# Attention with two dense layers behind it: the product with v of a group in one stretch behind the scores

## The chip, the core and the metric

One core of one Trainium2 chip runs the whole program. The metric is the device time of one execution in microseconds (us), as the median of three runs. The engines are TensorE (PE; its weight loads are PEld), VectorE (DVE), ScalarE (ACT), GpSimd (POOL) and SyncE (SP, which here issues DMAs).

## What is computed

Attention with a threshold on the scores, for 4 batches and 8 heads of 576 rows of 64, and two dense layers over the 2304 rows that come out:

```
scores = q @ k.T / sqrt(64)
scores = where(scores >= max(scores) - tau, scores, -1e9)
attn = exp(scores - max); attn = attn / (sum(attn) + 1e-9)
x = (attn @ v) as 2304 x 512
h = x @ w_in;  g = where(h >= 1, h, where(h <= -1, 0, (h + 1)**2 / 4));  x = g @ w_out
h = x @ w_in2; g = h * clip(h + 3, 0, 6) / 6;                             out = g @ w_out2
```

## The kernel before

Attention runs over 16 jobs, each one batch and two heads. A job has five blocks of query rows: four of 128 rows a head, and a last one with the 64 remaining rows of both heads. For each block `em_scores` computes the scores on TensorE (L285, four matmuls, each with 64 rows of the array and 288 columns, into the PSUM pairs P0 and P1). VectorE copies them out with their maximum (L297), ScalarE takes the exponential (L301), and VectorE applies the threshold and sums (L307). One step later `em_pt` transposes these probabilities on TensorE (L245) and ScalarE evicts them into the tile `Gf` (L328). Two steps later `em_tail` transposes the last 64 keys of both heads into `Gt` (L342, L346).

The five blocks make two groups: "a" is blocks 0 and 1 (256 columns), "b" is blocks 2 to 4 (320 columns). For a group `pv_chunk` multiplies with v in five chunks of 128 keys, and each chunk is two matmuls, one for each head (L362): head 0 writes partitions 0 to 63 of the PSUM bank Q1, head 1 partitions 64 to 127, so each uses 64 columns of the array. The first four chunks read `Gf`, the fifth `Gt`. A group is thus ten matmuls; all are float32, and the trace holds two records for each of them. The chunks wait in the list `pvq` and `pv_run(n)` takes up to n of them. After the fifth, ScalarE copies the result into `xu` (L368). Then `em_norm` transposes the row sums into a PSUM pair (L395, L397), VectorE multiplies `xu` by them (L399, L403), and the result goes to HBM (`xd`), from where the dense layers read it (`xst`). `em_norm` also loads the v of the job after the next (L237, L238).

`attention` walks over the 80 blocks, one step each, and yields between its parts. From the step on in which the first four jobs are through, each yield lets the loop outside lay a share of the first dense layer between (`dense1`: L486 is its first product, L548 its second, both float32r with 256 columns, from `em_h` and `em_part`). In the same time the weights are split into two parts on ScalarE, VectorE and GpSimd (L111 to L137, from w_raw to wih, wil, woh, wol). When attention is through, the dense layers go on alone with 512 columns.

The order on each engine is not the order of the code alone: the framework orders instructions when the program is built, by their dependencies and by when it thinks that each can start, and `after(mm, prev)` pins one TensorE instruction behind another. A chunk of the product with v is pinned, for head 0, behind the last entry of `pe_pins` (the first instruction of the last transposes or scores), and head 1 behind head 0.

Of the kernel before, what the change touches and what calls it, by code (L numbers as in the profile page):

```python
# [18 lines left out]
def kernel(  # L19
# [54 lines left out]
    def bank(tag):  # L74
        return ps.tile([128, 512], F32, tag=tag, name=tag)
# [20 lines left out]
    def after(ins, prev):  # L96
        if prev is not None:
            tc.add_manual_dep(ins.ins, prev.ins.name, mybir.DependencyInfo(
                mybir.DependencyClass.NoSync, mybir.DependencyReason.DATA), reason="pace")

    pe_pins = []
# [91 lines left out]
    AFTER = {1: "a", 4: "b"}  # L193
# [46 lines left out]
    def unit_bank():  # L240
        mode["s"] += 1
        return pair_bank(f"P{mode['s'] % 2}")

    def turn(out, in_, pin):
        x = T.transpose(out, in_, ident)  # L245
        if pin:
            pe_pins.append(x)

    def unit_q(j):
        if j >= NJ:  # L250
            return
        tm = unit_bank().rearrange("p e n -> p (e n)")
        for c in range(5):
            turn(tm[:, c * 128:(c + 1) * 128], qn[:, c, :], c == 0)
        load_q(j + 1)
        qt[j] = ap.tile([128, SEQ], F32, tag="qt", name="qt", bufs=2)
        S.activation(out=qt[j], in_=tm[:, 0:SEQ], func=ACTF.Copy, scale=taus[:, 1:2])
# [10 lines left out]
        S.activation(out=kt[j], in_=tm[:, 128 - TAIL:128 + MAIN + TAIL], func=ACTF.Copy)  # L268

    zt, gt, xu, p_t = {}, {}, {}, {}  # L270

    def em_scores(j, i):

        last = i == NBLK - 1

        if not last:
            mode["s"] += 1
        ss = [unit_bank() for _ in range(1 if last else 2)]
        prev = None
        c = slice(i * 128, i * 128 + (TAIL if last else 128))  # L280
        for x, (h, e) in enumerate(((0, 0), (1, 1), (0, 1), (1, 0)) if last else ((0, 0), (1, 0), (0, 1), (1, 1))):
            r = slice(h * D, (h + 1) * D)
            k0 = e * HS + (TAIL if last or h == 0 else 0)
            o = ss[0][h * TAIL:(h + 1) * TAIL, e, 0:HS] if last else ss[h][:, e, 0:HS]
            mm = T.matmul(o, qt[j][r, c], kt[j][r, k0:k0 + HS], start=True, stop=True, skip_group_check=True)  # L285
            after(mm, prev)
            prev = mm
            if x == 0:
                pe_pins.append(mm)
        nm = ap.tile([128, 2], F32, tag="nm", name="nm", bufs=3)  # L290
        th = ap.tile([128, 2], F32, tag="th", name="th", bufs=3)
        p = ap.tile([128, 2, 2, HS], F32, tag="p", name="p", bufs=3)
        if i == 0:
            zt[j] = ap.tile([128, 9], F32, tag="z", name="z", bufs=2)
        es = []
        for x, s in enumerate(ss):
            V.tensor_scalar(out=p[:, x], in0=s[:, :, 0:HS], scalar1=-1.0, scalar2=3e38,  # L297
                            op0=ALU.mult, op1=ALU.min, accum_out=nm[:, x:x + 1])
        for x, s in enumerate(ss):
            e = ap.tile([128, 2, HS], F32, tag="e", name="e", bufs=3)  # L300
            pins["S"] = S.activation(out=e, in_=p[:, x], func=ACTF.Exp, bias=nm[:, x:x + 1], scale=-1.0)  # L301
            es.append(e)
        n = len(ss)
        V.tensor_scalar(out=th[:, 0:n], in0=nm[:, 0:n], scalar1=taus[:, 0:1], scalar2=None, op0=ALU.add)
        for x, e in enumerate(es):
            z = ZCOL[x](i)
            V.scalar_tensor_tensor(out=p[:, x], in0=p[:, x], scalar=th[:, x:x + 1], in1=e,  # L307
                                   op0=ALU.is_le, op1=ALU.mult, accum_out=zt[j][:, z:z + 1])
        p_t[j, i] = p.rearrange("p h e n -> p (h e n)")
# [24 lines left out]
    def em_tail(j, i):  # L334

        p = p_t.pop((j, i))
        g, d0 = PARTS[i]
        t = gt[g, j][1]
        tl = bank("Q0" if mode["mlp"] else "Q3")
        if i < NBLK - 1:  # L340
            turn(tl[:, 0:128], p[:, MAIN:MAIN + 128], True)
            S.activation(out=t[:, d0:d0 + 128], in_=tl[:, 0:128], func=ACTF.Copy)  # L342
        else:
            turn(tl[0:TAIL, 0:128], p[:, MAIN:SEQ], True)
            for x in HEADS:
                S.activation(out=t[x * TAIL:(x + 1) * TAIL, d0:d0 + TAIL],  # L346
                             in_=tl[0:TAIL, x * TAIL:(x + 1) * TAIL], func=ACTF.Copy)

    o_t, pvq = {}, []

    def pv_chunk():

        j, g, c = pvq.pop(0)
        n, d0 = GROUPS[g]
        f, t = gt[g, j]
        if c == 0:
            if j not in xu:
                xu[j] = ap.tile([128, SEQ], F32, tag="xu", name="xu", bufs=2)
            o_t[j, g] = bank("Q1")
        o = o_t[j, g][:, 0:n]  # L360
        for h in HEADS:
            mm = T.matmul(o[h * D:(h + 1) * D], vn[j % 2][:, c, h, :], f[:, h, c] if c < 4 else t,  # L362
                          start=(c == 0), stop=(c == 4), skip_group_check=True)
            after(mm, pe_pins[-1] if h == 0 else prev)
            prev = mm
        if c == 4:
            del gt[g, j], o_t[j, g]
            S.activation(out=xu[j][:, d0:d0 + n], in_=o, func=ACTF.Copy)  # L368

    def pv_run(n):  # L370
        for _ in range(min(n, len(pvq))):
            pv_chunk()
# [3 lines left out]
    def pre_norm(j):  # L376
        z = zt.pop(j)
        rz = ap.tile([128, 9, 1], F32, tag="rz", name="rz", bufs=2)
        V.tensor_scalar(out=z, in0=z, scalar1=1e-9, scalar2=None, op0=ALU.add)
        V.reciprocal(out=rz[:, :, 0], in_=z)  # L380
        rb = ap.tile([128, 4, 2, 64], F32, tag="rb", name="rb")
        for h, z0 in ((0, 0), (1, 5)):
            G.tensor_scalar(out=rb[:, :, h, :], in0=rz[:, z0:z0 + 4, :].to_broadcast([128, 4, 64]),
                            scalar1=1.0, scalar2=0.0, op0=ALU.mult, op1=ALU.add)
        rbs[j] = (rz, rb)

    def em_norm(j):
        while any(x[0] == j for x in pvq):
            pv_chunk()
        load_v(j + 2)  # L390
        b, hp = jobs[j]
        rz, rb = rbs.pop(j)
        bm = unit_bank().rearrange("p e n -> p (e n)")
        for c in range(4):
            T.transpose(bm[:, c * 128:(c + 1) * 128], rb[:, c].rearrange("p h n -> p (h n)"), ident)  # L395
        bt = bm[:, 512:640]
        T.transpose(bt, rz[:, 4, :].to_broadcast([128, 128]), ident)  # L397
        x = xu.pop(j)
        V.tensor_tensor(out=x[:, 0:MAIN], in0=x[:, 0:MAIN], in1=bm[:, 0:MAIN], op=ALU.mult)  # L399
        nc.sync.dma_start(out=xd[b][:, hp, :], in_=x[:, 0:MAIN])  # L400
        for h in HEADS:
            r = slice(64 * h, 64 * h + 64)
            V.tensor_tensor(out=x[r, MAIN:SEQ], in0=x[r, MAIN:SEQ], in1=bt[r, 64 * h:64 * h + 64], op=ALU.mult)  # L403
        nc.sync.dma_start(out=xd[NB][:, hp, b * TAIL:(b + 1) * TAIL], in_=x[:, MAIN:SEQ])
# [3 lines left out]
    def attention():  # L408

        order = [(j, i) for j in range(NJ) for i in range(NBLK)]  # L410
        n = len(order)
        for t in range(n + 3):
            mode["t"] += 1
            mode["step"] = True
            j, i = order[t] if t < n else (NJ, t - n)
            if t < n:
                em_scores(j, i)
                yield
            if 2 <= t < n + 2:
                em_tail(*order[t - 2])  # L420
            pv_run(3)
            yield
            if i == 0 and j:
                pre_norm(j - 1)
            if i == 2 and j:
                em_norm(j - 1)
                done_jobs.add(j - 1)
                yield
            if i == 3:
                unit_q(j + 1)  # L430
                yield
            if i == 4:
                unit_k(j + 1)
                yield
            if 1 <= t < n + 1:
                j, i = order[t - 1]
                em_pt(j, i, 0)
                yield
            pv_run(2)
            if 1 <= t < n + 1:  # L440
                if i < NBLK - 1:
                    em_pt(j, i, 1)
                    yield
                if i in AFTER:
                    pvq.extend((j, AFTER[i], c) for c in range(5))


    xs, gs, acc, cnt = {}, {}, {}, {"h": 0, "a": 0}
# [157 lines left out]
    while o < len(outs):  # L606
        n = len(steps)
# [138 lines left out]
    for _ in attention():  # L746
# [11 lines left out]
        while credit > 0:  # L758
            c = next(part1)
# [98 lines left out]
```

## Time and profile before

| | |
|---|---|
| median of three runs | 1183.13 us (1182.69 to 1183.19) |
| the profiled execution | 1181.81 us, span 1180.0 us |
| mean granted TensorE clock | 0.993 |
| TensorE matmuls busy | 1133.5 us (96%) |
| weight loads busy | 907.5 us (77%) |
| ScalarE, VectorE, GpSimd busy | 631.2, 581.4, 412.3 us |

Busy is the time in which at least one instruction of the engine was in work; matmuls overlap, so their own durations say less than the distance from one start to the next. The rows below are of that one execution.

### The profile page before, as it was taken

How to read it: one execution, taken by the hardware profiler on the slowest of the kernel's cores; microseconds unless marked ns; L12 is line 12 of the kernel's file. 1: busy time of each engine (PE TensorE's matmuls, PEld its weight loads, DVE VectorE, ACT ScalarE, POOL GpSimd, SP SyncE). 2: the span in 40 equal slices, each digit the busy share in tenths (PEclk: the TensorE clock that was granted, in tenths of full speed). 3: DMA queues.
4: the chain of work that ended last, by engine and by line, in shares of the span. 5: the costliest groups of instructions: out<-in, count | busy, mean ns of one | idle time of the engine just before them, and what ended most of it. 6: DMA issues, size and time to landing. Idle time of an engine off the chain costs nothing.

```text
span 1180.0 us, 17986 instructions
## 1 busy us (share of the span) xinstructions
PE 1133.5 (96%) x6680; PEld 907.5 (77%) x6680; DVE 581.4 (49%) x1208; ACT 631.2 (53%) x1234; POOL 412.3 (35%) x388
## 2 busy tenths in 40 slices
PE   8888799989999999999999999999999999999998
PEld 5555576667777777787888988888888888888886
DVE  5888876765565555535543666556631121121111
ACT  5666777755566656655664776645532232233222
POOL 0322663511111011113762756657833222222221
PEclk9999999999999999999999999999999999999999
DMA  5333344322212112004422245443210010010000
GB/s 132 88 93 92 108 139 126 109 62 71 69 52 60 40 41 58 21 20 124 146 90 72 87 147 160 149 146 98 72 50 9 1 60 8 1 46 1 18 1 36
DMA packets 110056, 85.59 MB, mean 73 GB/s; under 512 B 66704, under 2 KB 93840, under 8 KB 109968
## 3 DMA queue, kind: packets, MB, share of 16 engines
q1 hardware_dynamic: 108608, 84.14, 24.3%
q8 instruction: 53, 0.87, 0.3%
q10 hardware_dynamic: 1360, 0.30, 0.1%
q14 instruction: 35, 0.29, 0.1%
HBM read 66.06 MB, written 18.35 MB: 72 GB/s over the span
## 4 chain that ended last, share of the span: by engine, by line
PE 82%; ACT 5%; DVE 5%; DMA 4%; issue 2%; POOL 1%; ACTq 0%; SPq 0%; DVEq 0%; POOLq 0%
PE Q L486 33%; PE P L528 26%; PE Q L548 6%; PE Q L362 6%; PE P L285 5%; PE Q L245 5%; DVE p L297 2%; ACT e L301 1%; DVE p L307 1%; DMA xst<-xd 1%; PE P L245 1%; DMA xd<-xu 1%; ACT Gf L328 1%; DMA w_raw<-in_moe_w_out_dram 1%; ACT r L495 1%
## 5 line engine op out<-in xcount | busy, mean ns | idle before, releaser
L504 POOL TENSOR_TENSOR gl<-r,gh 128x512 fp32r<-128x512 f32 (+1 forms) x190 | 205.8, 1083 | 587.0 <-ACT gh L503 574.5
L486 PE MATMUL Q<-xh,wih 128*128 128x512 f32 (+1 forms) x760 | 265.2, 350 | 5.2 <-DVE r L497 3.9
L486 PE MATMUL Q<-xl,wih 128*128 128x512 f32 (+1 forms) x760 | 257.5, 339 | 0.6 <-DVE xl L470 0.5
L486 PE MATMUL Q<-xh,wil 128*128 128x512 f32 (+1 forms) x760 | 257.4, 339 | 0.0
L500 DVE SCALAR_TENSOR_TENSOR r<-r,Q 128x512 f32<-128x512 f32 (+1 forms) x80 | 50.7, 634 | 249.1 <-ACT r L499 248.9
L486 PEld LDWEIGHTS Q<-xh,wih 128*128 128x128 f32 x760 | 144.6, 190 | 37.2 <-issue 10.3
L503 ACT ACTIVATE gh<-r 128x512 fp32r<-128x512 f32 (+1 forms) x190 | 99.8, 525 | 119.6 <-PE P L528 53.1
L486 PEld LDWEIGHTS Q<-xl,wih 128*128 128x128 f32 x760 | 144.6, 190 | 16.7 <-DVE xl L470 1.0
L486 PEld LDWEIGHTS Q<-xh,wil 128*128 128x128 f32 x760 | 144.4, 190 | 15.4
L297 DVE TENSOR_SCALAR_CACHE_REDUCE p<-P 128x576 f32<-128x576 f32 x144 | 104.1, 754 | 70.8 <-PE Q L245 54.3
L307 DVE SCALAR_TENSOR_TENSOR p<-p,th,e 128x576 f32<-128x576 f32 x144 | 125.5, 886 | 25.0 <-ACT e L301 18.3
L245 PE MATMUL Q<-ident,p 128*128 128x128 f32 (+1 forms) x656 | 112.9, 287 | 19.2 <-ACT Gf L328 9.6
L301 ACT ACTIVATE e<-p,nm 128x576 f32<-128x576 f32 x144 | 109.6, 773 | 38.2 <-DVE p L297 36.9
L499 ACT ACTIVATE r<-Q,three 128x512 f32<-128x512 f32 (+1 forms) x80 | 51.4, 643 | 143.7 <-PE Q L486 140.6
L245 PEld LDWEIGHTS Q<-ident,p 128*128 128x128 f32 (+1 forms) x656 | 74.9, 142 | 57.5 <-ACT Gf L328 14.9
L497 DVE SCALAR_TENSOR_TENSOR r<-r,Q 128x256 f32<-128x256 f32 (+1 forms) x110 | 55.0, 500 | 119.0 <-ACT r L496 118.5
L285 PE MATMUL P<-kt,qt 64*128 64x288 f32 (+1 forms) x640 | 103.7, 432 | 10.3 <-DVE p L297 4.4
L528 PE MATMUL P<-woh,gh 128*128 128x512 f32 x288 | 111.9, 390 | 0.6 <-DVE ob L586 0.6
L528 PE MATMUL P<-wol,gh 128*128 128x512 f32 x288 | 112.2, 390 | 0.0
L528 PE MATMUL P<-woh,gl 128*128 128x512 f32 x288 | 111.0, 390 | 0.0
L130 POOL TENSOR_TENSOR w_c<-w_c,w_raw 128x512 int32<-128x512 int32 x64 | 90.5, 1414 | 39.8 <-DVE w_c L128 33.2
L328 ACT ACTIVATE Gf<-Q 128x512 f32<-128x512 f32 x128 | 75.0, 590 | 47.6 <-PE Q L245 47.4
(83 smaller groups left out, 1870.7 us busy)
## 6 DMA issues: line engine op xcount, KB each, us to landing
w_raw<-in_moe_w_in_dram SPq DMA_DIRECT2D x32, 512.0 KB, 3.9
w_raw<-in_moe_w_out_dram SPq DMA_DIRECT2D x32, 512.0 KB, 3.7
xst<-xd SPq DMA_DIRECT2D x32, 256.0 KB, 3.4
kn<-in_k_dram SPq DMA_DIRECT2D x32, 128.0 KB, 2.6
vn<-in_v_dram SPq DMA_DIRECT2D x32, 128.0 KB, 2.6
xd<-xu SPq DMA_DIRECT2D x16, 256.0 KB, 2.5
x2p<-ob SPq DMA_DIRECT2D x16, 256.0 KB, 2.5
x2d<-ob SPq DMA_DIRECT2D x16, 256.0 KB, 3.7
```

Of the source, the lines that this page charges most:

```text
L130: x = G.tensor_tensor(out=c.bitcast(I32), in0=c.bitcast(I32), in1=r, op=ALU.add)
L245: x = T.transpose(out, in_, ident)
L285: mm = T.matmul(o, qt[j][r, c], kt[j][r, k0:k0 + HS], start=True, stop=True, skip_group_check=True)
L297: V.tensor_scalar(out=p[:, x], in0=s[:, :, 0:HS], scalar1=-1.0, scalar2=3e38, op0=ALU.mult, op1=ALU.min, accum_out=nm[:, x:x + 1])
L301: pins["S"] = S.activation(out=e, in_=p[:, x], func=ACTF.Exp, bias=nm[:, x:x + 1], scale=-1.0)
L307: V.scalar_tensor_tensor(out=p[:, x], in0=p[:, x], scalar=th[:, x:x + 1], in1=e, op0=ALU.is_le, op1=ALU.mult, accum_out=zt[j][:, z:z + 1])
L328: S.activation(out=f[:, h, :, d0:d0 + 128], in_=tm.rearrange("p (c n) -> p c n", c=4), func=ACTF.Copy)
L362: mm = T.matmul(o[h * D:(h + 1) * D], vn[j % 2][:, c, h, :], f[:, h, c] if c < 4 else t, start=(c == 0), stop=(c == 4), skip_group_check=True)
L486: mm = T.matmul(h, l[:, kk * 128:(kk + 1) * 128], r, start=(x == 0), stop=(x == 3 * KD - 1))
L503: x = S.activation(out=gh, in_=r, func=ACTF.Copy)
L504: y = G.tensor_tensor(out=gl, in0=r, in1=f32(gh), op=ALU.subtract)
L528: T.matmul(a, l, r, start=(first and x == 0), stop=(last and x == 2))
```

## The change

The chunks of a group are entered in the list one step later, after `em_tail` of its last block, so that all five are there at once. `pv_run(5)` stands right behind `em_scores`, ahead of the yield, in place of `pv_run(3)` and `pv_run(2)` in two later places of the step. The pin of head 0 is now the last matmul of the scores (`last_score`), or the last matmul of the chunk before. The loop has one step more for it.

```diff
@@ -268,6 +268,7 @@
     zt, gt, xu, p_t = {}, {}, {}, {}
+    last_score = [None]
 
@@ -287,6 +288,7 @@
             if x == 0:
                 pe_pins.append(mm)
+        last_score[0] = prev
         nm = ap.tile([128, 2], F32, tag="nm", name="nm", bufs=3)
@@ -361,8 +363,9 @@
                           start=(c == 0), stop=(c == 4), skip_group_check=True)
-            after(mm, pe_pins[-1] if h == 0 else prev)
+            after(mm, last_score[0] if h == 0 else prev)
             prev = mm
+        last_score[0] = prev
@@ -409,16 +412,19 @@
-        for t in range(n + 3):
+        for t in range(n + 4):
             mode["t"] += 1
             mode["step"] = True
             j, i = order[t] if t < n else (NJ, t - n)
             if t < n:
                 em_scores(j, i)
-                yield
+            pv_run(5)
+            yield
             if 2 <= t < n + 2:
-                em_tail(*order[t - 2])
-            pv_run(3)
+                jt, it = order[t - 2]
+                em_tail(jt, it)
+                if it in AFTER:
+                    pvq.extend((jt, AFTER[it], c) for c in range(5))
             yield
@@ -436,13 +442,10 @@
                 em_pt(j, i, 0)
                 yield
-            pv_run(2)
             if 1 <= t < n + 1:
                 if i < NBLK - 1:
                     em_pt(j, i, 1)
                     yield
-                if i in AFTER:
-                    pvq.extend((j, AFTER[i], c) for c in range(5))
```

What this does to the order on TensorE is shown at two places. The first is group b of the first job, in the stretch with attention alone, before (P is a score, Q with p a transpose of probabilities, Q with Gf or Gt the product with v; x6 is six matmuls in a row):

```order
L285 MATMUL P_414<-kt,qt 128x288
L362 MATMUL Q_442<-Gf,vn_96 64x320 x6
L245 MATMUL Q_451<-ident,p 128x128 x4
L362 MATMUL Q_442<-Gf,vn_96 64x320 x2
L362 MATMUL Q_442<-Gt,vn_96 64x320 x2
L245 MATMUL Q_462<-ident,p 128x128 x4
L245 MATMUL Q_492<-ident,p 128x128
```

The same group now, where the product stands one block of scores later:

```order
L286 MATMUL P_457<-kt,qt 128x288
L364 MATMUL Q_474<-Gf,vn_96 64x320 x8
L364 MATMUL Q_474<-Gt,vn_96 64x320 x2
L245 MATMUL Q_510<-ident,p 128x128 x4
L245 MATMUL Q_516<-ident,p 128x128 x4
L398 MATMUL P_499<-ident,rb 128x128 x4
L400 MATMUL P_499<-ident,rz 128x128
```

All ten matmuls are in one stretch behind the scores, and the transposes for the normalisation (L398) come soon after. The second place is group b of the eighth job, in the stretch where dense work lies between, before:

```order
L245 MATMUL Q_3022<-ident,p 64x128
L362 MATMUL Q_3026<-Gf,vn_97 64x320 x6
L245 MATMUL Q_3035<-ident,p 128x128 x4
L362 MATMUL Q_3026<-Gf,vn_97 64x320 x2
L362 MATMUL Q_3026<-Gt,vn_97 64x320 x2
L395 MATMUL P_3077<-ident,rb 128x128 x4
```

and now (L551 is the dense product that was L548):

```order
L551 MATMUL Q_2859<-gh,wol_2644 128x256
L364 MATMUL Q_3058<-Gf,vn_97 64x320
L245 MATMUL Q_3022<-ident,p 64x128
L364 MATMUL Q_3058<-Gf,vn_97 64x320 x7
L245 MATMUL Q_3028<-ident,p 128x128 x4
L364 MATMUL Q_3058<-Gt,vn_97 64x320 x2
L398 MATMUL P_3077<-ident,rb 128x128 x4
```

The six and four have become one, seven and two, and the product doesn't stand behind scores.

At the end of attention, between the last matmul of the product with v and the first matmul with 512 columns, there are 33 narrow dense matmuls before and 24 now. Counted over the whole order, the 32 groups stand on TensorE like this (a stretch is a run of matmuls of one group with nothing between; a lone head more is one that has no partner in its stretch, counted in pairs of them; an end at scores is a stretch that begins right behind scores or ends right ahead of them):

| groups | stretches before, now | pairs before, now | ends at scores before, now |
|---|---|---|---|
| first 8, attention alone | 16, 8 | 41, 40 | 9, 8 |
| next 9 (108 to 280 us before) | 19, 29 | 46, 54 | 2, 9 |
| last 15 (280 to 535 us before) | 30, 47 | 75, 92 | 0, 9 |

A pair here is what two heads side by side take, and a lone head counts as one pair too: five of the eight added in the middle line, and eight of the seventeen in the last, are of 256 columns, the others of 320.

## Rows read from the trace of the kernel before

**Rows 1.** Busy us (records) of PE, PEld, DVE, ACT, POOL; clock; DMA share, GB/s.

```profile
0.00:108.00 108.00, 92.32 (x612) 58.44 (x613) 79.97 (x213) 68.78 (x138) 25.16 (x41) 0.97 0.38 100
108.00:280.00 172.00, 151.62 (x1084) 114.24 (x1084) 123.47 (x287) 121.59 (x261) 75.65 (x76) 0.98 0.38 109
280.00:535.00 255.00, 250.78 (x1871) 194.57 (x1871) 136.23 (x376) 154.14 (x337) 34.91 (x51) 1.00 0.16 44
```

**Rows 2.** TensorE's timeline: start, us, instruction, records [idle before].

```profile
99.00 1.24 PE L285 MATMUL P<-kt,qt 64*128 64x288 f32 x8
100.17 1.83 PE L362 MATMUL Q<-Gf,vn 128*64 128x320 f32 x12
101.93 1.24 PE L285 MATMUL P<-kt,qt 64*128 64x288 f32 x8
...
106.68 1.24 PE L285 MATMUL P<-kt,qt 64*128 64x288 f32 x8
107.85 0.66 PE L245 MATMUL Q<-ident,p 128*128 128x128 f32 x4
...
116.07 0.65 PE L362 MATMUL Q<-Gf,vn 128*64 128x256 f32 x4
116.55 0.60 PE L362 MATMUL Q<-Gt,vn 128*64 128x256 f32 x4
117.08 1.19 PE L285 MATMUL P<-kt,qt 64*64 64x288 f32 x8
```

**Rows 3.** TensorE's timeline at a group that stands in three pieces.

```profile
276.63 0.65 PE L362 MATMUL Q<-Gf,vn 128*64 128x256 f32 x4
277.11 0.59 PE L362 MATMUL Q<-Gt,vn 128*64 128x256 f32 x2
277.64 0.39 PE L486 MATMUL Q<-xh,wih 128*128 128x256 f32 x1
...
278.94 0.28 PE L486 MATMUL Q<-xl,wih 128*128 128x256 f32 x1
279.06 0.28 PE L486 MATMUL Q<-xh,wil 128*128 128x256 f32 x1
279.27 0.65 PE L362 MATMUL Q<-Gt,vn 128*64 128x256 f32 x2
279.84 0.38 PE L548 MATMUL Q<-gh,woh 128*128 128x256 f32 x1
280.07 0.28 PE L548 MATMUL Q<-gl,woh 128*128 128x256 f32 x1
```

**Rows 4.** TensorE's timeline at a lone head with 320 columns.

```profile
78.50 0.75 PE L362 MATMUL Q<-Gf,vn 128*64 128x320 f32 x2
79.18 0.66 PE L245 MATMUL Q<-ident,p 128*128 128x128 f32 x4
```

**Rows 5.** Waits of TensorE, 20 to 108: total, times, longest.

```profile
PE Q L245 <- DVE p L307: 5.3, 6, 1.0
```

**Rows 6.** Waits of TensorE, 108 to 280 us.

```profile
PE Q L245 <- ACT Gf L328: 8.8, 5, 3.6
...
PE P L285 <- DVE xu L403: 3.1, 4, 0.9
```

**Rows 7.** Chain that ended last, 118 to 136: start, us, what.

```profile
123.94 4.70 DMA w_raw<-in_moe_w_out_dram
...
130.00 0.49 ACT Gf L328
```

**Rows 8.** Busy time by short stretch, columns as in the first group.

```profile
131.00:133.00 2.00, 2.00 (x14) 2.00 (x13) 0.46 (x3) 1.66 (x4) 1.39 (x3) 0.63 0.56 166
```

**Rows 9.** Chain that ended last, at the end of attention.

```profile
534.89 0.45 ACT xu L368
...
541.96 4.22 PE Q L486 x12
```

**Rows 10.** Waits of SP's DMA queue, 20 to 540 us.

```profile
SPq L237 <- PE Q L362: 166.6, 14, 20.3
```

## The prediction

> **What bounds the kernel now.** I read first the busy time of each engine by stretch [rows 1]. The kernel has four stretches: attention alone (0 to 108 us), attention with the first dense products laid between its steps (108 to 280 and 280 to 535), and dense products alone. The change touches the first three. From 280 to 535 TensorE is without work for 4.2 us of 255: there every added microsecond of TensorE shows. From 0 to 108 it lacks 15.7 us and from 108 to 280 20.4 us; there other engines decide part of the time. Then I read who is waited for. In the first stretch TensorE's transposes wait for VectorE's probabilities, 5.3 us in six waits [rows 5]. In the second they wait 8.8 us in five for the eviction of earlier transposes, the longest 3.6 us, and the scores wait 3.1 us in four for the normalisation that holds their PSUM pair [rows 6]. The chain to the longest wait goes through a weight transfer of 4.70 us and ends in such an eviction on ScalarE [rows 7].
>
> **What a stretch of the product with v costs.** The prices come from starts in TensorE's timeline. Each matmul of the program leaves two records, so a chunk (two heads) leaves four. At 256 columns four matmuls take 1.01 us up to the next instruction (116.07 to 117.08), three matmuls also 1.01 us (276.63 to 277.64), and one 0.57 us (279.27 to 279.84) [rows 2, 3]. So the two heads run side by side in the two halves of the columns, a lone head costs as much as a pair, and a stretch costs 0.44 us a pair and 0.13 us once. At 320 columns six take 1.76 us (100.17 to 101.93) and one 0.68 us (78.50 to 79.18) [rows 2, 4]: 0.54 us a pair and 0.14 us once. Around a stretch two more things are paid. The dense matmul ahead takes 0.21 us to the next start in place of 0.12 us (279.06 and 278.94), and the first one behind takes 0.23 us (279.84 to 280.07) [rows 3]: 0.09 and 0.11 us. Behind scores the entry is free: scores take 1.17 us whether a product follows (99.00 to 100.17) or a transpose (106.68 to 107.85) [rows 2].
>
> So one break more that leaves a lone head on each side costs 0.57 + 0.09 + 0.11 = 0.77 us at 256 columns and 0.68 + 0.20 = 0.88 us at 320. A break between whole chunks costs 0.13 + 0.20 = 0.33 us. An end of a stretch that lies at scores gets back the 0.20 us.
>
> **What the change does, by the order on TensorE.** It doesn't do one thing. The first 8 groups (attention alone) stand in two stretches each before and in one stretch behind the scores now. The other 24 groups stand in 49 stretches before, nearly all 6 + 4 matmuls, and in 76 now: the pin to the last score holds the place of the first matmul alone, dense work is laid between, and the usual pattern is 1 + 7 + 2, with a lone head at the first break. So the change lengthens TensorE's work where TensorE is fullest.
>
> First stretch: eight stretches fewer at 0.14 + 0.09 us, 1.8 us, and one lone head fewer (one group was split 1 + 9), 0.54 us: 2.4 us less work. But the product with v now stands in the same steps as the key transposes and the normalisation, and three of five steps have none: a heavy step waits for TensorE, a light one for VectorE. The gain is at most 2.4 + 5.3 = 7.7 us, if the product covers all waits for the probabilities; the loss is at most 3.1 us, if the scores of all four jobs wait for the normalisation as the four in [rows 6] do (0.78 us each). I take half of the saved work, -1.2 us, because VectorE's chain sets about half of these steps.
>
> Second stretch, 9 groups: ten stretches more, eight of them with a lone head more (five at 256, three at 320): 5 x 0.77 + 3 x 0.88 + 2 x 0.33 = 7.2 us; seven more ends lie at scores, -1.4 us: +5.8 us of work. There is 20.4 us of idle time to take it. Bounds: all of it hidden, and the 3.6 us wait gone together with at least 0.7 us of low clock behind it (granted 0.63 from 131 to 133, a part of it at 1.2 GHz, after TensorE had waited) [rows 8]: -4.3 us; or nothing hidden and four more waits for the normalisation: 5.8 + 3.1 = +8.9 us. I take half of the work, +2.9 us, since the waits there come in a few long pieces and much of the work stands elsewhere.
>
> Third stretch, 15 groups: seventeen stretches more, each with a lone head more (eight at 256, nine at 320): 8 x 0.77 + 9 x 0.88 = 14.1 us; nine ends at scores, -1.8 us: +12.3 us. Bounds: all idle time takes some of it, 12.3 - 4.2 = +8.1 us; or the scores of eight jobs wait 0.78 us each, +18.5 us. I take +11.8 us, as the idle time there is many short pieces.
>
> End of attention: the last normalised block goes through HBM before the wide products start, 7.1 us from ScalarE's copy to the wide product [rows 9]. Between the last product with v and the first wide matmul 33 narrow dense matmuls stood, now 24: nine less at 0.12 us cover 1.1 us less. Bounds 0 and 2.2 us (nothing of it waited for; or the lost time doubled by a low clock).
>
> Moved too, and costed at nothing: ScalarE's copy of the product (16 + 16, count unchanged) comes one step later, just ahead of the normalisation; if that slack is gone, the price is the 0.78 us above. The loads of v on SP's queue wait for the product of the group [rows 10], now later by part of a step; behind them stand the store of the same normalisation, which needs that product anyway, and loads of q and weights. The v is used a job later, which covers them; if a weight load is caught there, the price is a wait like the one of 3.6 us. The dense work itself is the same in number.
>
> Sum: -1.2 + 2.9 + 11.8 + 1.1 = +14.6 us. The profiled execution took 1181.81 us, so 1196.4; the median of the runs is 1.3 us above that execution, so **1197.7 us**.
>
> **Rivals.** (a) The added work is hidden. If TensorE had room in the third stretch too, only the first stretch and the end count: -1.2 + 1.1, 1183.0 us. Against it: 4.2 us idle in 255, and the dense matmuls follow each other every 0.12 us. The Trainium skill, "Perfetto Trace Analysis", section "Identifying the Most-Contended Engine", says that a busy share of matmuls doesn't tell how near TensorE is to its limit and that the busy share of weight loads does; in the third stretch that is 194.57 of 255 us, 76%, which by this rule leaves room. The timeline speaks against it here, since a break lengthens the start-to-start times themselves. 5 in 100.
>
> (b) Faster: the middle belongs to the weights. The chain there runs through weight transfers and their conversion [rows 7], so longer steps could meet the weights just when they are ready, and all 20.4 us of idle time could go: 5.8 - 20.4 = -14.6 us there, and with the rest 1183.1 - 1.2 - 14.6 + 11.8 + 1.1 = 1180.2 us. It decides only if more than 17.5 of the 20.4 us go; waits for evictions and the normalisation are part of them and stay. 4 in 100.
>
> (c) A new wait: the scores of every job wait for the normalisation, since the product now ends just ahead of it. At 0.78 us for 16 jobs this adds 12.4 us, 1210.1 us. For it: four of the first scores after 108 us do so already; against it: from 280 us on the 4.2 us of idle time leave room for short waits alone, since dense work stands between. 9 in 100.
>
> **Chances and range.** The forecast, slower by 5 to 23 us, has 82 in 100; with (c) slower has 91, the same (within 0.2%, 2.4 us, about what the measurement can tell) 5, faster 4. The ends of all bounds together would be -3.9 and +32.7 us, but they don't fall together. From 1188 to 1207 leaves out (a), (b), most of (c) and some of the forecast.
>
> **What would show it.** Right: in the third stretch the product with v in pieces of 2, 14 and 4 records, the lone head taking 0.57 or 0.68 us, the attention's end near 549 us in place of 535, and the dense part as long as before. In the first stretch one piece of 20 records behind the scores and little change in time. Wrong would be: the middle shorter by more than its added work, with the waits for the evictions gone; long waits of scores for the normalisation after 280 us; or pieces whose lone heads find a partner.

## The result

The changed kernel takes 1195.3 us as the median of five runs (1194.1 to 1197.4), beside 1182.7 us before (1179.7 to 1183.2, five runs): ratio 1.011 [1.0094, 1.0126], so 13.0 us slower (11.1 to 14.9). The forecast was 1197.7 us and slower. Below, a difference between kernels is made from their ratios; 0.001 is 1.18 us.

Landmarks that part the stretches of the profiled execution:

| landmark, us | before | after | later by |
|---|---|---|---|
| first dense matmul | 108.4 | 112.2 | 3.7 |
| first scores of job 9, counted from 0 (near the bound at 280 us) | 274.9 | 280.7 | 5.8 |
| last start of the product with v | 534.4 | 547.6 | 13.2 |
| first wide matmul | 542.0 | 555.1 | 13.1 |
| end of the span | 1180.0 | 1193.4 | 13.4 |

So the first stretch adds 3.7 us, the middle 2.1, the third 7.4, and the end of attention and the dense part nothing. These landmarks don't part equal work, however. In the changed kernel the middle holds twelve dense matmuls more (462 for 450; three of them stood in the third stretch before, nine behind it), two matmuls of a group's product more (1.0 us in their pieces) that stood in the third, and two transposes more that stood in the first. At 0.12 us a dense matmul and 0.5 us for the transposes, as an estimate, the four parts at equal work are about 4, -1, 9 and 1 us. Busy time by stretch, with the columns of [rows 1]:

```profile
0.00:111.80 111.80, 90.85 (x611) 59.44 (x611) 80.37 (x220) 71.40 (x140) 24.76 (x41) 0.94 0.37 95
111.80:284.00 172.20, 157.08 (x1092) 115.89 (x1089) 123.00 (x281) 121.85 (x261) 73.18 (x77) 0.98 0.38 110
284.00:547.90 263.90, 261.49 (x1874) 197.47 (x1873) 136.31 (x376) 154.17 (x335) 33.74 (x50) 1.00 0.16 42
```

TensorE's idle time grew in the first stretch from 15.7 to 21.0 us. It shrank in the middle from 20.4 to 15.1 us and in the third from 4.2 to 2.4 us: there the added time is work. TensorE's timeline of the changed kernel shows that work, columns as in [rows 2]; L364 is the product with v:

```profile
312.95 0.28 PE L551 MATMUL Q<-gh,wol 128*128 128x256 f32 x1
313.16 0.65 PE L364 MATMUL Q<-Gf,vn 128*64 128x256 f32 x2
313.73 0.87 PE L245 MATMUL P<-ident,kn 128*128 128x128 f32 x6
...
315.15 0.28 PE L551 MATMUL Q<-gh,wol 128*128 128x256 f32 x1
315.36 1.94 PE L364 MATMUL Q<-Gf,vn 128*64 128x256 f32 x14
317.23 0.38 PE L489 MATMUL Q<-xh,wih 128*128 128x256 f32 x1
...
320.39 0.28 PE L489 MATMUL Q<-xh,wil 128*128 128x256 f32 x1
320.60 0.65 PE L364 MATMUL Q<-Gt,vn 128*64 128x256 f32 x4
321.18 0.66 PE L245 MATMUL Q<-ident,p 128*128 128x128 f32 x4
```

One group stands in three pieces of 2, 14 and 4 records, which take 0.57, 1.87 and 0.58 us up to the next start, 3.02 us. In the first stretch the same ten matmuls do stand in one piece behind the scores:

```profile
21.80 1.19 PE L286 MATMUL P<-kt,qt 64*64 64x288 f32 x8
22.92 1.95 PE L364 MATMUL Q<-Gf,vn 128*64 128x256 f32 x16
24.70 0.60 PE L364 MATMUL Q<-Gt,vn 128*64 128x256 f32 x4
25.23 0.87 PE L245 MATMUL P<-ident,kn 128*128 128x128 f32 x6
```

From 22.92 to 25.23 they take 2.31 us, 0.71 us less. What one waits for there changed as well. The waits of the changed kernel from 20 to 108 us (total, times, longest), which answer to [rows 5]; L299 is VectorE's copy of the scores with their maximum:

```profile
DVE p L299 <- PE P L286: 11.6, 8, 3.0
...
PE P L286 <- DVE p L299: 6.0, 6, 1.5
...
PE Q L245 <- DVE p L309: 2.7, 3, 1.0
```

Transposes wait less for the probabilities (2.7 us for 5.3), but the scores now wait 6.0 us for VectorE to free their PSUM (1.3 us in two before), and VectorE waits 11.6 us for scores (9.2 us in ten before). After 108 us, TensorE's waits answer to [rows 6]:

```profile
PE P L286 <- DVE xu L406: 6.0, 4, 3.9
...
PE Q L245 <- ACT Gf L330: 1.1, 2, 0.8
```

The wait for evictions went from 8.8 to 1.1 us and the one of scores for the normalisation from 3.1 to 6.0 us; after 284 us the latter is 0.2 us in one wait.

### The profile page after: what moved, and what is told of

Its sections match the earlier page's. It is cut to its first block, busy times and chain, and to the rows that moved or that the text cites. A ratio compares the mean times of both kernels' runs of the same rounds, so it can differ in the third digit from the quotient of the medians.

```text
span 1193.4 us, 17997 instructions
## 1 busy us (share of the span) xinstructions
PE 1147.4 (96%) x6680; PEld 912.5 (76%) x6680; DVE 581.9 (49%) x1208; ACT 632.3 (53%) x1234; POOL 405.5 (34%) x388
## 4 chain that ended last, share of the span: by engine, by line
PE 86%; DVE 6%; ACT 4%; DMA 3%; issue 1%; ACTq 0%; SPq 0%; DVEq 0%
PE Q L489 33%; PE P L531 26%; PE Q L364 7%; PE Q L551 7%; PE P L286 6%; PE Q L245 5%; DVE p L299 2%; DVE p L309 2%; PE P L245 1%; ACT e L303 1%; DMA xd<-xu 1%; DMA xst<-xd 1%; ACT Gf L330 0%; PE P L398 0%; DVE xl L473 0%
## 5 line engine op out<-in xcount | busy, mean ns | idle before, releaser
L299 DVE TENSOR_SCALAR_CACHE_REDUCE p<-P 128x576 f32<-128x576 f32 x144 | 104.0, 754 | 76.0 <-PE Q L245 59.9
L286 PE MATMUL P<-kt,qt 64*128 64x288 f32 (+1 forms) x640 | 106.3, 440 | 18.2 <-DVE p L299 9.1
L245 PEld LDWEIGHTS Q<-ident,p 128*128 128x128 f32 (+1 forms) x656 | 75.1, 143 | 53.6 <-issue 15.1
L531 PE MATMUL P<-wol,gh 128*128 128x512 f32 x288 | 112.2, 390 | 0.0
L130 POOL TENSOR_TENSOR w_c<-w_c,w_raw 128x512 int32<-128x512 int32 x64 | 87.5, 1367 | 42.2 <-DVE w_c L128 32.2
```

Of the source, the lines that this page charges most:

```text
L130: x = G.tensor_tensor(out=c.bitcast(I32), in0=c.bitcast(I32), in1=r, op=ALU.add)
L531: T.matmul(a, l, r, start=(first and x == 0), stop=(last and x == 2))
```

## The experiments

The theory after the result: the time is lost because the 24 later groups stand in 76 pieces, at the prices of the prediction; the first stretch loses through its new step, and the middle hides part of both. The rivals: it is the later step as such, not the pieces, that costs; or the middle hides nothing.

**One half of the change at a time.** `new_way(j)` chooses the jobs for which chunks are entered, run and pinned in the new way; the other jobs keep the old places.

```diff
+    def new_way(j):
+        return j < HP        # the second run: j >= HP
...
-            after(mm, pe_pins[-1] if h == 0 else prev)
+            after(mm, (last_score[0] if new_way(j) else pe_pins[-1]) if h == 0 else prev)
...
+            pv_run(5, True)
...
+                if it in AFTER and new_way(jt):
+                    pvq.extend((jt, AFTER[it], c) for c in range(5))
+            pv_run(3, False)
```

> The change for the first four jobs alone: their 8 groups in one stretch behind the scores, the other 24 as before (6 + 4). Theory 1 (the first stretch loses by itself, because the product now stands in the same steps as the key transposes and the normalisation, and VectorE is waited for): 3.7 us more, near 1186.4 us. Rival (the first stretch only shifts work, and the weights that are further on at its end give the time back in the middle): 1182 to 1184 us. By the prediction's own term, -1.2 us: 1181.5 us.

Measured: 1180.9 us, ratio 0.9984 [0.9966, 1.0001]. The first dense matmul is 2.2 us late (110.66 us), the first scores of job 9 are 1.7 us early (273.19). So the middle gives back what the first stretch lost, and more.

> The change for the jobs from the fifth on alone: 8 groups as before, 24 groups in the pieces of the changed kernel (mostly 1 + 7 + 2). Theory 1 (the pieces with lone heads cost 7.4 us in the third stretch and about 2 us in the middle): near 1192 us. Rival (first and later stretches hang together, so that the first stretch as before takes nothing off): near 1195 us.

Measured: 1193.1 us, ratio 1.0088 [1.0070, 1.0106]. The late groups alone make most of the loss. The two halves sum to 8.5 us (10.4 less 1.9) and the whole to 13.0; the uncertainties taken together are some 3.5 us. A reading that fits, but is not shown, is that the idle time of the middle can be used once: by the lost time of the first stretch or by the added work.

**The stretch that the change describes.** Only the chunk of `Gt` has to wait for the eviction of the last transposes. Put first in the list, it no longer holds up the end of a stretch; a higher priority holds the ten matmuls together.

```diff
-        if c == 0:
+        if c == 4:
...
-            mm = T.matmul(o[h * D:(h + 1) * D], vn[j % 2][:, c, h, :], f[:, h, c] if c < 4 else t,
-                          start=(c == 0), stop=(c == 4), skip_group_check=True)
+            with tc.high_priority():
+                mm = T.matmul(o[h * D:(h + 1) * D], vn[j % 2][:, c, h, :], f[:, h, c] if c < 4 else t,
+                              start=(c == 4), stop=(c == 3), skip_group_check=True)
...
+                if it in AFTER:
+                    pvq.extend((jt, AFTER[it], c) for c in (4, 0, 1, 2, 3))
```

> The changed kernel with each group's chunk that reads Gt first and the ten matmuls at high priority: all 32 groups stand in one stretch of ten, at the same step as in the changed kernel. Theory 1 (the pieces are what costs after 108 us): 25 stretches and one lone head fewer than the kernel before there, -3.8 us inside them and 0 to -6.6 us around them, and +3.7 us in the first stretch: 1176 to 1183 us. Rival (the later step costs, by the normalisation that then waits and holds the scores): 1190 to 1195 us, like the changed kernel.

Measured: 1179.2 us, ratio 0.9970 [0.9958, 0.9982], 16.6 us below the changed kernel with every product in the same step. All 32 groups stand in one piece, of 2.31 us (256 columns) or 2.84 us (320). The pieces cost, not the later step.

> The first four jobs as before, all later groups in one stretch of ten as in the run with ten everywhere. Theory 1: -3.8 us inside the stretches and 0 to -6.6 us around them against the kernel before: 1172 to 1179 us, faster than both kernels. Rival (the later step costs): 1187 to 1192 us.

Here the first four jobs stay as before and the others are as in the run above. Measured: 1176.1 us, ratio 0.9941 [0.9918, 0.9964], 7.0 us faster than before: the best version of this study. Its timeline at one group:

```profile
309.23 0.75 PE L289 MATMUL P<-kt,qt 64*128 64x288 f32 x2
309.90 0.65 PE L369 MATMUL Q<-Gt,vn 128*64 128x256 f32 x4
310.39 1.90 PE L369 MATMUL Q<-Gf,vn 128*64 128x256 f32 x16
312.21 0.66 PE L245 MATMUL Q<-ident,p 128*128 128x128 f32 x4
```

From 309.90 to 312.21 the ten matmuls take 2.31 us. The piece of scores ahead is a block's first one alone, which comes back below.

**A cut alone, and a lone head alone.** Both kernels are the one above with its late stretches cut by transposes, 23 of 24 groups: behind the second chunk (four and six matmuls), or in the middle of the third (five and five, a lone head on each side; `ODD` is true for this one).

```diff
-            pv_run(5, True)
+            if split:
+                pv_chunk()
+                pv_chunk()
+                if ODD:
+                    pv_chunk((0,))
...
+                if split:
+                    last_score[0] = pe_pins[-1]
+                    if ODD:
+                        pv_chunk((1,))
+                    pv_run(3, True)
```

> The run with ten late, with 23 of its 24 late groups cut into four and six matmuls by transposes (whole chunks on both sides). Against that run (1176.1 us) theory 1 (a stretch more costs 0.13 us inside and up to 0.2 us around it) gives 3 to 8 us more: 1179 to 1184 us. Rival (what surrounds a stretch costs nothing, since the kind of work changes there anyway): 3 us more, 1179 us.

> As the run with four and six, but cut into five and five, inside a chunk, so that a lone head stands on each side; place and number of the cuts are the same. Theory 1 (a lone head costs a pair's time): 12 cuts at 0.44 us and 11 at 0.54 us, 11.2 us more than four and six, of which about 2 us may be hidden in the middle: 9 to 11 us more. Rival (a cut costs by the change of kind alone, wherever it lies): no difference.

Measured: 1179.0 us, ratio 0.9976 [0.9964, 0.9989], and 1183.7 us, ratio 1.0016 [1.0004, 1.0028]. The same group in TensorE's timeline, cut in four and six:

```profile
312.59 0.65 PE L372 MATMUL Q<-Gt,vn 128*64 128x256 f32 x4
313.07 0.60 PE L372 MATMUL Q<-Gf,vn 128*64 128x256 f32 x4
313.60 0.33 PE L245 MATMUL Q<-ident,p 128*128 128x128 f32 x1
...
318.50 1.51 PE L372 MATMUL Q<-Gf,vn 128*64 128x256 f32 x12
319.95 0.38 PE L580 MATMUL Q<-gh,woh 128*128 128x256 f32 x1
```

and cut in five and five:

```profile
311.85 0.65 PE L372 MATMUL Q<-Gt,vn 128*64 128x256 f32 x4
312.33 1.03 PE L372 MATMUL Q<-Gf,vn 128*64 128x256 f32 x6
313.29 0.66 PE L245 MATMUL Q<-ident,p 128*128 128x128 f32 x4
...
318.19 1.51 PE L372 MATMUL Q<-Gf,vn 128*64 128x256 f32 x10
319.63 0.38 PE L581 MATMUL Q<-gh,woh 128*128 128x256 f32 x1
```

Four and six take 1.01 + 1.45 us, five and five 1.44 + 1.44: the lone head adds 0.42 us (0.52 at 320 columns), 10.8 us for 23 groups. The ratios differ by 0.0040, 4.7 us, where 9 to 11 were expected. The rest was hidden in the middle: the first scores of job 9 stand at 284.0 and 283.9 us in the two, and from there to the last product with v five and five takes 5.8 us longer. A cut between whole chunks costs 4.1 us for 23, 0.18 us each, surroundings included (the stretch itself 0.13 to 0.15); the 4.1 us are uncertain by some 3 us.

**The first stretch: long pieces in the old step.** The kernel of before, with the new pin for the first four jobs only. Four of their eight groups now stand in one piece, the others as eight and two or nine and one.

```diff
+        last_score[0] = prev
...
-            after(mm, pe_pins[-1] if h == 0 else prev)
+            after(mm, (last_score[0] if j < HP else pe_pins[-1]) if h == 0 else prev)
```

> The kernel before with the new pin for the first four jobs alone, at the old step: four of their eight groups in one stretch of ten, the others 8 + 2 or 9 + 1. It tells the step apart from the one stretch. Theory 1 (the later step, with key transposes and normalisation in it, costs the 2.2 to 3.7 us at the end of the first stretch): the first dense matmul near 108.4 us as before, in all 1181 to 1183 us. Rival (a long stretch holds up the transposes and scores behind it, wherever it stands): the first dense matmul near 110.7 us.

Measured: 1187.9 us, ratio 1.0044 [1.0027, 1.0061], 5.2 us more than before. The first dense matmul is 9.0 us late (117.43) in the profiled execution, which at 1191.6 us is the slowest of the four. Both expectations missed: a long piece behind the scores loses time in the old step too, so the later step isn't needed for a loss. The waits from 20 to 108 us:

```profile
DVE p L299 <- PE P L286: 15.1, 13, 2.6
...
PE Q L245 <- DVE p L309: 8.0, 5, 2.1
```

VectorE waits 15.1 us for scores (9.2 before) and the transposes 8.0 us for probabilities (5.3 in [rows 5]): the two engines wait for each other in turn. Up to the first scores of job 4 (105.45 us, 99.00 before) TensorE is idle for 6.8 us more, and that makes the 6.45 us of delay there. The rest is mostly the clock. From those scores to the first dense matmul, before and here, with the columns of [rows 1]:

```profile
99.00:108.42 9.42, 8.43 (x59) 4.69 (x58) 8.13 (x21) 5.21 (x12) 3.92 (x5) 1.00 0.39 101
105.45:117.43 11.98, 10.46 (x58) 5.74 (x58) 6.79 (x19) 5.57 (x12) 2.49 (x4) 0.72 0.31 81
```

For the same matmuls TensorE is busy for 2.0 us longer, at a granted clock of 0.72 in place of 1.00, and idle for 0.5 us more.

> The first four jobs as in the run with early contiguous, all later groups in one stretch of ten. Theory 1 (the parts add up): the time of the run with ten late, 1176.1 us, less what the early part gains alone, 0 to 2 us: 1174 to 1176 us. Rival (a gain in the first stretch is taken back in the middle by the weights): 1176 to 1178 us.

The same, with ten in the late groups. Measured: 1183.0 us, ratio 1.0002 [0.9986, 1.0018], a miss: 7.2 us more than the run with ten in the late groups alone. In the profiled execution, again the slowest (1187.3 us), the first dense matmul is 9.1 us later than in that run, at a granted clock of 0.90 up to there (0.98 in that run), and the middle takes 2.0 us longer. In both traces the middle gives back nothing of such a loss.

**The price list on another order.** The changed kernel with the priority alone, the chunk of `Gt` still last: 59 late pieces for 76.

```diff
-            mm = T.matmul(o[h * D:(h + 1) * D], vn[j % 2][:, c, h, :], f[:, h, c] if c < 4 else t,
-                          start=(c == 0), stop=(c == 4), skip_group_check=True)
+            with tc.high_priority():
+                mm = T.matmul(o[h * D:(h + 1) * D], vn[j % 2][:, c, h, :], f[:, h, c] if c < 4 else t,
+                              start=(c == 0), stop=(c == 4), skip_group_check=True)
```

> The changed kernel with a higher priority on the product with v alone, and the chunk of Gt still last: the 24 later groups stand in 59 stretches in place of 76 (13 in two pieces of eight and two, 11 in three of one, seven and two; a lone head more in those 11, all of 256 columns). This tries the price list on an order that it was not made from. Theory (0.18 us a cut, 0.42 us a lone pair, as the runs with four and six and with five and five gave, the middle stretch absorbing all of its lone pairs): against the run with ten everywhere, 1179.2 us, 35 stretches more make 6.3 us and 11 lone pairs 4.6 us, less some 5 us of both that the middle hides: 1182 to 1188 us, ratio 1.002 to 1.005, the last start of the product with v at 537 to 544 us. Rival 1, that what costs is the place late in the step (the Gt chunk stands where it stands in the changed kernel): as the changed kernel, 1193 to 1196 us. Rival 2, that the lone heads alone cost and even cuts nothing: 1179 to 1182 us, last start 533 to 536 us.

Measured: 1191.1 us, ratio 1.0069 [1.0051, 1.0087]. All three expectations missed. Against ten everywhere it is 11.7 us; the list gives 6.3 + 4.6 = 10.9 us with nothing hidden. That these are near each other is luck, as the two traces show. The first stretch, which the list leaves out, is 2.3 us longer, at a granted clock of 0.95 for 0.98. The middle is 3.2 us longer, but holds twelve dense matmuls (1.4 us) and most of a group's product (1.7 us) that stand behind it with ten everywhere; at equal work it takes nothing more, where the list gives 4.0 us. So the middle did hide its part. The third stretch is 5.9 us longer (256.3 and 262.1), at equal work 9.0 us, where the list gives 22 cuts and 7 lone heads, 6.9 us. Over the same 15 groups the product takes 6.3 us more (38.92 and 45.25), near the list, but the scores take 2.5 us more as well (45.97 us for 43.51, 280 records each), which no term of the list holds. The reason stands in its timeline:

```profile
319.02 0.75 PE L286 MATMUL P<-kt,qt 64*128 64x288 f32 x2
319.70 0.65 PE L365 MATMUL Q<-Gt,vn 128*64 128x256 f32 x4
```

The product stands between the first matmul of a block's scores and the other three. That lone one takes 0.68 us up to the next start, and the other three 1.17 us (321.58 to 322.75), as long as all four. After 284 us scores are cut into one and three in 7 blocks here, in 4 with ten everywhere, in 3 before.

> The run with ten in the late groups (1176.1 us) without the higher priority, the chunk of Gt first: 20 late groups in one stretch, 4 in two or three (seven stretches and some three lone heads more). Theory: it is the order of the five chunks that frees the stretch from the wait for Gt, the priority does little; 5 stretches at 0.18 and 3 lone pairs at 0.45 make +2.3 us: 1177 to 1180 us, ratio 0.995 to 0.998. Rival, that the gain of 0.6 per cent came from the priority (TensorE's other work moved with it): as before, 1182 to 1185 us, ratio 1.000 to 1.002.

```diff
+        first, end = (4, 3) if new_way(j) else (0, 4)
...
-                          start=(c == 0), stop=(c == 4), skip_group_check=True)
-            after(mm, pe_pins[-1] if h == 0 else prev)
+                          start=(c == first), stop=(c == end), skip_group_check=True)
+            after(mm, (last_score[0] if new_way(j) else pe_pins[-1]) if h == 0 else prev)
...
+                if it in AFTER and new_way(jt):
+                    pvq.extend((jt, AFTER[it], c) for c in (4, 0, 1, 2, 3))
```

Measured: 1180.5 us, ratio 0.9981 [0.9971, 0.9991]. It differs from the run with the late groups changed (1.0088) by the order of the five chunks alone: its late groups stand in 28 pieces in place of 75, and that is worth 12.7 us. That the chunk of `Gt` breaks the stretches because the framework expects its operand late fits this, but the times by which the framework orders are not on record. Against ten with the priority it is 4.7 us slower, where 1 to 4 were expected. In the traces the product with v takes 1.85 us more (its cuts and lone heads), and the scores after job 9's first ones 1.0 us more (44.3 for 43.3 us, 280 records each), since three blocks of them stand in pieces of one, two and one. The last 1.8 us are within what the runs leave uncertain.

**The first stretch: the later step without the long piece.** The first four jobs in the new step, each group cut in six and four by transposes; the others as before.

```diff
-            pv_run(5)
+            pv_run(3, True)
+            cut = bool(pvq) and new_way(pvq[0][0])
...
+                if cut:
+                    em_pt(*order[t - 1], 0)
+                    last_score[0] = pe_pins[-1]
+                    pv_run(2, True)
```

> The first four jobs in the later step of the change, but each stretch of ten cut in six and four by transposes of the block before; the 24 other groups as before. Theory (the long stretch right behind the scores makes VectorE and TensorE wait for each other; the later step costs nothing): first dense matmul at 108.0 to 109.3 us (108.42 before, 110.66 with the long stretch in the same step), time 1180 to 1184 us, ratio 0.998 to 1.001. Rival (the later step, with the key transposes and the normalisation in the same step, costs the 2.2 us too): first dense matmul at 110.5 us or later, and the same ratio, since the middle gives a loss of this size back either way. A ratio above 1.002 would speak against the middle giving it back.

Measured: 1182.7 us, ratio 0.9995 [0.9983, 1.0006]. The first dense matmul stands at 109.57 us, between the two expectations. Job 4's first scores stand at 98.07 us, earlier than before (99.00) and than in the four traces with the long piece in this step (99.56 to 101.86). But the clock differs too:

```profile
0.00:98.07 98.07, 81.00 (x559) 51.78 (x559) 71.98 (x196) 65.46 (x128) 21.69 (x37) 1.00 0.39 100
```

The granted clock up to job 4 is 1.00 here and 0.97 before; of the four it is 0.98 in the two at 99.56 and 99.94 us and 0.95 in the two at 101.44 and 101.86. The matmuls up to there are the same in number in all of them, so part of the gain of this run is the clock, and how much of the loss is the long piece stays open. TensorE's idle time up to there is 14.7 us before, 17.1 here, and 19.0 to 19.4 with the long piece, which speaks for both the piece and the step. From job 4's first scores to the first dense matmul the clock is full in four traces: 9.4 us before, 10.5 with ten everywhere and with the priority alone, with four records less, and 11.5 here, with five records more than before. So at the end of the stretch some 1 us comes with the later step, whether the group is cut or not.

## Why the prediction was right

It was right in sign and size, by terms whose errors cancelled: at equal work the parts are about 4, -1, 9 and 1 us, where it had -1.2, 2.9, 11.8 and 1.1. That the sum came out within 2 us (14.6 and 13.0) is luck; that the pieces of the third stretch decide its sign is not. By its own steps:

- **First stretch, -1.2 us: wrong.** It took 3.7 us more, above its own upper bound of 3.1. The work did shrink (TensorE busy 92.3 to 90.9 us), but "I take half of the saved work" took a gain where the heavy and light steps that the paragraph names cost more than that: TensorE's idle time grew by 5.3 us. The two runs of the old step with long pieces show that a long piece behind the scores is enough for such waits; the run with the group cut shows that at the end of the stretch the later step costs too. Part of the 3.7 us goes with the clock. The new order ran four times under the profile (once with the chunk of `Gt` first), with the first dense matmul at 110.1, 110.7, 112.2 and 112.4 us. The granted clock up to there is 0.94 in the changed kernel; in the run with the early half alone, whose order up to there is the same, it is 0.97, as before, and the loss 2.2 us. Ten microseconds of the changed kernel and of the run with the early half alone, columns as in [rows 1]; the clock is the number behind GpSimd's busy time:

```profile
74.00:84.00 10.00, 7.90 (x31) 4.83 (x30) 5.88 (x18) 6.64 (x15) 1.39 (x3) 0.50 0.15 33
```

```profile
74.00:84.00 10.00, 6.71 (x47) 4.23 (x45) 7.79 (x24) 8.12 (x17) 1.39 (x3) 1.00 0.15 33
```

  In the first TensorE stands at its lower level, 1.2 GHz, and gets through 31 records; in the second, at 2.4 GHz, through 47. Ahead of the fall it had stood for 1.75 us waiting for ScalarE's eviction of q; in the run with ten everywhere it stood there for 1.52 us and the clock stayed at 1.00, and before the change the clock fell (0.50 from 74 to 76 us) behind waits of 1.21 and 0.53 us; the length of such a wait alone doesn't tell. Kernels with the old order had the first dense matmul at 108.4 to 109.1 us, so the new one costs some 1 to 4 us here.
- **Middle, +2.9 us: near in number (2.1), by luck.** The 2.1 us are work that stood elsewhere before; at equal work the middle takes nothing more. The work inside the stretches grew as priced: over the same nine groups the product with v takes 5.3 us more (24.85 and 30.17, each piece from its start to the next start, idle time left out), where the list gives 5 x 0.57 + 3 x 0.68 + 2 x 0.13 = 5.2 us. Idle time fell by 5.3 us, so it took all of this, where "I take half of the work" let half of it show. What left was the wait for evictions; the wait for the normalisation grew.
- **Third stretch, +11.8 us: right in cause, too large (7.4, at equal work 8.8).** The price inside was right: over the same 15 groups the product with v went from 41.16 to 51.89 us, 10.7 us more, and the list gives 8 x 0.57 + 9 x 0.68 = 10.7. The term that failed is the 0.20 us around a break: less its credits it was 1.6 us in the forecast and came to nothing. The old breaks stood between transposes and dense work, and paid too (entries behind transposes 25 before, 8 now; behind dense matmuls 7 and 36). The transposes take 2.2 us less, and the dense matmuls together 1.9 us more at equal counts. The run with four and six, where a cut costs 0.18 us in all, fits that. Idle time gave another 1.8 us back; the prediction gave it 0.5.
- **End of attention, +1.1 us: right at equal work, though not seen between the landmarks (-0.1).** From the last start of the product with v to the first wide matmul it is 7.5 us both times. The chain of the changed kernel there:

```profile
547.33 0.71 PE Q L364 x4
...
548.07 0.45 ACT xu L371
...
554.38 0.64 ACT xh L472
...
555.07 1.62 PE Q L489 x3
```

  It is 7.0 us from ScalarE's copy to the wide product, as in [rows 9] (7.1): the trip through HBM ends the gap either way. The nine dense matmuls that left it now stand ahead of the last product with v, where at 0.12 us each they lengthen the stretches by about 1.1 us.
- **Rivals.** Hidden work (a) fell: the third stretch has a weight-load share of 75% (197.5 of 263.9 us) and still grew by 7.4 us. The Trainium skill's rule in "Perfetto Trace Analysis", section "Identifying the Most-Contended Engine", goes by MFU as well, which isn't worked out here; its busy share of weight loads alone doesn't decide this stretch. That the middle gains (b) holds in part for the early half alone (3.9 us shorter), not for the whole change. The wait of all jobs for the normalisation (c) fell: after 284 us it is 0.2 us.

Open: how much of an added microsecond the middle hides. At equal work it hid the added product of this change and of the priority-only run, the lone heads of five and five, and the loss of the early half, but nothing of the 9 us of the early long pieces. Open too is how the loss of the first stretch parts between the long piece, the later step and the clock.

## What to carry to other kernels

Price a reordering by the order that comes out, not by what the code asks for: here 24 groups that were asked for in one stretch each came out in 76, and handing one chunk over first was worth 12.7 us. Where two matmuls share the array side by side, cut between pairs or not at all, since a lone one costs a pair. Where two engines take turns, a longer uninterrupted piece on one can starve the other, even with less work in all. Before a stretch of two traces is compared, count the work in it and look at the clock: an order that moves work across a landmark, or one trace at a lower clock, can look like a gain or a loss.

## What was not expected of the hardware

- A lone half-array matmul costs a pair wherever it stands: 0.57 us at 256 columns behind dense work, and 0.42 us more than in company in the cut stretches. The same holds for scores, which use half of the array's rows: one alone takes 0.68 us, three as long as four (1.17 us).
- A stretch of ten takes 2.31 or 2.84 us whatever stands before and behind it, in nearly all of 32 places; five pairs at 0.44 and 0.13 once, or 0.54 and 0.14, give 2.33 and 2.84.
- The new order's first stretch ended between 110.1 and 112.4 us from trace to trace, with ten microseconds at 1.2 GHz in one trace and none of them in another. A landmark of a single trace is good to some 2 us there, not to the 0.1 us of its digits.
